# Temporaries of a weight conversion in a PSUM buffer, its last subtraction on VectorE, and a new list schedule

## The chip, the cores and the metric

One core of a Trainium2 chip runs the whole kernel. The metric is the device time of one execution in microseconds. Five engines take part, each with its own instruction queue: TensorE (PE, its weight loads PEld), VectorE (DVE), ScalarE (ACT), GpSimd (POOL) and SyncE (SP), which here issues nearly all DMAs and passes semaphores on.

## What is computed

A convolution whose weights depend on the position, then a small feed-forward layer with a rational activation. All arrays are float32 except for the two weight matrices, whose 64-bit words are loaded as they are and converted in the kernel.

```python
w = exp(weight_gen - max) / (sum + 1e-9)             # (4, 4096, 8 heads, 7 taps)
attn[b, s, h, :] = sum over k of w[b, s, h, k] * x_pad[b, s + k, h, :]   # 8 heads x 24 = 192
h = attn @ w_in                                      # (16384, 192) @ (192, 2048)
P = a0 + a1*h + a2*h**2 + a3*h**3
Q = 1 + |b0|*|h| + |b1|*h**2
out = (P / (Q + 1e-6)) @ w_out                       # (16384, 2048) @ (2048, 192)
```

## The kernel before

The 16384 rows are cut into 32 chunks of 512 rows, the 2048 columns of the inner layer into 8 slots of 256, so 256 slots in all. For each chunk GpSimd makes the seven taps and adds them (`tap`, `tap_add`), TensorE transposes the result into an h buffer (`tr`), ScalarE casts it (`cast`, L645), VectorE subtracts the cast to get the low part (`rest`, L654), and SP copies both to other partitions (`both`, L664 to xd and L670 to xs). Chunk 0 goes a shorter way, with its taps on VectorE.

A slot is then: TensorE's first product into an h buffer (`m1`, L700, 18 matmuls over high and low parts), on ScalarE the absolute value (`v1`, L734), a square (`z1`, L738), a Ln (L751) and an Exp (L754), on VectorE three operations (`d1` L742, `w1` L746, `gg` L758), of which the last writes g and so frees the h buffer, and on TensorE the second product, called gather here (`m2`, L713), in two halves that add into the accumulator acc. Between the two halves a semaphore instruction on SP (`relay`, L775) passes the accumulator on; it stands in SP's queue like a DMA issue. At a chunk's end ScalarE evicts acc (`ev`, L813). PSUM holds three h buffers and acc.

While the first slots run, the weights are still being converted (`unit`): 14 blocks, A0 to A3 and B0, B1 of w_in (512 words a row each) and W0 to W7 of w_out (384 words). A block is loaded as raw; ScalarE takes its magnitude (`ua1`, mag) and its rounding (`ua2`, rnd); VectorE shifts the high words (`ub1`, L393, tile t), joins sign and exponent (`ub2`, L398, tile w), adds the rounding (`ub3`, L403) and clears tiny values (`ub4`, L408), which for the W blocks writes wo. For A and B blocks ScalarE casts w to the high part wh (`uh`, L436) and the low part wl is w minus wh (`uw`, L440), on VectorE for A0 and B0, on GpSimd for the other four. Tiles t and w lie in SBUF, one t and two w. Slots 2j and 2j+1 of chunks 0 and 1 wait for block Aj, slots 0 to 3 and 4 to 7 also for B0 and B1, the gather of slot i for Wi.

The order on each engine is worked out at build time by a list scheduler (`arrange`). Each operation is an `Op` with an engine, a planned duration, a key, what it depends on, the buffers that it takes and uses. At each step every engine proposes, among its operations that can start within `PATIENCE` of its earliest one, that of the lowest key, and the engine that can start first is served. The tables `OFF` (offsets of a slot's or a chunk's steps), `KEY` and `LOADS` (the blocks) set the keys; `PITCH` is the planned time of a slot. An operation of VectorE with `lock=True` is planned as shutting out GpSimd, and GpSimd it. On the chip each engine simply goes through its row of instructions and waits for semaphores.

Of the kernel before, what the change touches and what calls it, by code (L numbers as in the profile page):

```python
# [14 lines left out]
ALU = mybir.AluOpType  # L15
# [6 lines left out]
P = 128  # L22
# [5 lines left out]
N = Q * P  # L28
# [9 lines left out]

BUFS = {
# [3 lines left out]
}  # L43

PITCH = 4.8545
OFF = {
    "g": 13.51, "ex": 4.89, "ln": 3.41, "v": 12.93, "z": 5.73, "d": 7.19, "w1": 3.82, "m2": 3.16,
    "aft": 0.41, "step": 1.43, "cast": 0.61, "rest": -18.71, "dup": 12.06, "lead": 13.14,
    "w": 46.44, "wW": 10.17, "one": -7.23, "ahead": 52.98, "ul": -53.2,
}  # L50
KEY = {
    "B0": -29.4, "A0": -28.0, "W0": 32.8, "A1": 30.0, "W1": 12.93, "W2": 43.45, "W3": 40.29,
    "B1": 40.0, "A2": 50.17, "W4": 52.64, "W5": 52.8, "A3": 52.8, "W6": 62.0, "W7": 69.16,
}
LOADS = (
    "B0", "A0", "W0", "A1", "W1", "W2", "W3", "B1", "A2", "W4", "W5", "A3", "W6", "W7",
# [26 lines left out]
def hand(a, b):  # L83
    if a.land is not None:
        return 0.1
    if a.eng == b.eng:
        return 0.0
    return 0.22 if a.eng == "PE" else 0.08


PATIENCE = 0.346


def arrange(ops, place):
    users, newest = {}, {}
    for i, o in enumerate(ops):
        o.seq = i
        o.left = len(o.deps)
        for d in o.deps:
            d.outs.append((o, True))  # L100
        for t in o.takes:
            if t[0] not in LOOSE:
                if t[0] in newest:
                    newest[t[0]].outs.append((o, False))
                    o.left += 1
                newest[t[0]] = o
        for t in o.takes + o.uses:
            users.setdefault(t, []).append(o)
    engines = ("PE", "ACT", "DVE", "POOL", "SP")
    free = dict.fromkeys(engines, 0.0)  # L110
    ready = {e: [] for e in engines}
    for o in ops:
        if not o.left:
            ready[o.eng].append(o)
    taken = {}
    order = []
    pool_busy = (0.0, 0.0)
    pipe = 0.0

    def room(o):  # L120
        t = 0.0
        for tile_id in o.takes:
            held = taken.setdefault(tile_id[0], [None] * BUFS[tile_id[0]])
            first = None
            for k, past in enumerate(held):
                at = freed(past, o) if past is not None else 0.0
                if at is not None and (first is None or at < first[0]):
                    first = at, k
            if first is None:
                return None  # L130
            t = max(t, first[0])
            place[tile_id] = first[1]
        return t

    def freed(tile_id, o):
        t = 0.0
        for u in users[tile_id]:
            if u.start is None:
                return None
            t = max(t, (u.start + u.land if u.land is not None else u.end) + hand(u, o))  # L140
        return t

    while len(order) < len(ops):
        best = None
        for e in engines:
            found = []
            for o in ready[e]:
                r = room(o)
                if r is not None:
                    found.append((max(free[e], o.ready, r), o))  # L150
            if not found:
                continue
            low = min(s for s, _ in found) + PATIENCE
            s, o = min(
                (x for x in found if x[0] <= low),
                key=lambda x: (
                    x[1].key + (max(0.0, pool_busy[1] - x[0]) * LOCK if x[1].lock else 0.0),
                    x[1].seq,
                ),
            )  # L160
# [37 lines left out]
def kernel(  # L198
# [10 lines left out]
    nc = tc.nc  # L209
# [87 lines left out]
    def sg_():  # L297
# [8 lines left out]
        unit_, inv, sign, op=ALU.mult), [o_r1])  # L306
# [45 lines left out]

    ready_w = {}

    def unit(u):
        kind, j = u[0], int(u[1])
        base = KEY[u]
        t = {}
        width = 2 * D if kind == "W" else U
        cost = 0.75 if kind == "W" else 1.0  # L360
# [28 lines left out]
                out=t["rnd"], in_=t["lo"].bitcast(U32), func=ACTF.Identity, scale=2.0 ** -29)  # L389

        def ub1():
            t["t1"] = tiled(("t1", u), [P, width], I32)
            nc.vector.tensor_scalar(  # L393
                t["t1"], t["hi"], 3, 0x3FFFFFF8, op0=ALU.logical_shift_left, op1=ALU.bitwise_and)

        def ub2():
            t["w"] = tiled(("w", u), [P, width], I32)
            nc.vector.scalar_tensor_tensor(  # L398
                out=t["w"], in0=t["hi"], scalar=-0x40000000, in1=t["t1"], op0=ALU.bitwise_and,
                op1=ALU.bitwise_or)  # L400
# [11 lines left out]
        issue = {"A": 0.9, "B": 0.9, "W": 0.45}[kind]  # L412
        raw, mag, rnd, t1, w = ((k, u) for k in ("raw", "mag", "rnd", "t1", "w"))
        o = op("SP", issue, OFF["ul"] + LOADS.index(u), ul, takes=[raw], land=512.0 * cost)
        p1 = op("ACT", 0.67 * cost, base, ua1, [o], takes=[mag], uses=[raw])
        p2 = op("ACT", 0.66 * cost, base, ua2, [o], takes=[rnd], uses=[raw])
        o = op("DVE", 0.42 * cost, base + 0.5, ub1, [o], takes=[t1], uses=[raw], lock=True)
        o = op("DVE", 0.69 * cost, base + 1.0, ub2, [o], takes=[w], uses=[raw, t1], lock=True)
        o = op("DVE", 0.69 * cost, base + 1.5, ub3, [o, p2], uses=[w, rnd], lock=True)
        o = op("DVE", 0.69 * cost, base + 2.0, ub4, [o, p1], uses=[w, mag], lock=True)  # L420
        if kind == "W":
            ready_w[u] = [o]
            return
# [1 line left out]
        if kind == "A":  # L425
            high, low = (v[:, 0:2, 2 * j:2 * j + 2, :].rearrange("p b n c -> p b (n c)")
                         for v in (wh, wl))
        else:
            high, low = (v[:, 2:3, 4 * j:4 * j + 4, :].rearrange("p b n c -> p b (n c)")
                         for v in (wh, wl))  # L430

        def words_of():
            return t["w"].bitcast(FP32).rearrange("p (b f) -> p b f", b=2 if kind == "A" else 1)
# [2 lines left out]
            nc.scalar.copy(out=high, in_=words_of())  # L436

        def uw():
            eng = nc.vector if u in FAST else nc.gpsimd
            eng.tensor_tensor(low, words_of(), high.bitcast(FP32), op=ALU.subtract)  # L440

        oh = op("ACT", 0.62, base + 3.0, uh, [o], uses=[w])
        if u in FAST:
            ol = op("DVE", 0.69, base + 4.0, uw, [oh], uses=[w], lock=True)
        else:
            ol = op("POOL", 1.27, base + 4.0, uw, [oh], uses=[w])
        ready_w[u] = [oh, ol]

    FAST = ("A0", "B0")
    for u in LOADS:  # L450
        unit(u)

# [371 lines left out]
    for n in range(NSLOT):  # L824
# [3 lines left out]
        slot(n, made[c][0], made[c][1], made[c][2])  # L828

    order = arrange(ops, place)  # L830
    with tc.manual_schedule():
        nc.scalar.preload_act_table_set("natural_log_exp_and_others")
# [136 lines left out]
```

## Time and profile before

| | us |
|---|---|
| median of 3 runs | 1323.15 (1322.0 to 1325.54) |
| the profiled execution | 1321.83 |
| its span, first to last instruction | 1320.0 |

| engine | busy us | share of the span |
|---|---|---|
| TensorE matmuls | 1268.7 | 96% |
| VectorE | 1156.0 | 88% |
| ScalarE | 1140.9 | 86% |
| GpSimd | 895.3 | 68% |

The shares are averages over a head of some 100 us, in which chunk 0 is prepared and the weights are converted, and a long even part. A share says what an engine did, not what it waited for; for the latter there are the rows of single instructions with their idle time. Operations of one line can have two sizes (384 and 512 words), so a mean over a line mixes them.

### The profile page before, as it was taken

How to read it: one execution, taken by the hardware profiler on the slowest of the kernel's cores; microseconds unless marked ns; L12 is line 12 of the kernel's file. 1: busy time of each engine (PE TensorE's matmuls, PEld its weight loads, DVE VectorE, ACT ScalarE, POOL GpSimd, SP SyncE). 2: the span in 40 equal slices, each digit the busy share in tenths (PEclk: the TensorE clock that was granted, in tenths of full speed). 3: DMA queues.
4: the chain of work that ended last, by engine and by line, in shares of the span. 5: the costliest groups of instructions: out<-in, count | busy, mean ns of one | idle time of the engine just before them, and what ended most of it. 6: DMA issues, size and time to landing. Idle time of an engine off the chain costs nothing.

```text
span 1320.0 us, 30705 instructions
## 1 busy us (share of the span) xinstructions
PE 1268.7 (96%) x13082; PEld 1150.2 (87%) x13082; DVE 1156.0 (88%) x975; ACT 1140.9 (86%) x1162; POOL 895.3 (68%) x582
## 2 busy tenths in 40 slices
PE   7549999999999999999999999999999999999998
PEld 5438998999999999999999899999899999999997
DVE  7998988888889989888888898988888988889874
ACT  4649989988899899989989899998899899889985
POOL 2585898766767876666787666688766668866300
PEclk9869999999999999999999999999999999999999
DMA  7322122232112222211222222123222212221100
GB/s 186 98 69 65 51 67 75 79 79 78 48 43 67 78 78 79 79 44 39 75 78 79 79 49 62 47 79 78 79 78 50 54 56 78 78 78 46 45 13 15
DMA packets 46291, 89.07 MB, mean 67 GB/s; under 512 B 5426, under 2 KB 27976, under 8 KB 46148
## 3 DMA queue, kind: packets, MB, share of 16 engines
q1 hardware_dynamic: 45860, 87.05, 24.2%
q8 instruction: 104, 1.70, 0.5%
q14 instruction: 39, 0.32, 0.1%
q10 hardware_dynamic: 288, 0.00, 0.0%
HBM read 41.40 MB, written 12.58 MB: 41 GB/s over the span
## 4 chain that ended last, share of the span: by engine, by line
PE 87%; DVE 6%; ACT 3%; SPq 2%; issue 1%; DMA 1%; ACTq 0%; DVEq 0%
PE acc L713 48%; PE h L700 38%; PE h L632 1%; SPq L664 1%; ACT av L754 1%; DVE w L403 1%; DVE av L742 1%; DVE w L398 1%; DVE t L393 1%; DMA x<-in_x_dram 1%; DVE g L758 1%; DVE wo L408 1%; ACT av L751 1%; ACT av L734 0%; SPq L670 0%
## 5 line engine op out<-in xcount | busy, mean ns | idle before, releaser
L713 PE MATMUL acc<-wo,g 64*128 64x192 f32 x8192 | 723.1, 325 | 14.9 <-DVE g L758 10.1
L713 PEld LDWEIGHTS acc<-wo,g 64*128 64x128 f32 x8192 | 680.8, 187 | 48.0 <-SPq L775 12.1
L742 DVE SCALAR_TENSOR_TENSOR av<-av,cf 128x1024 f32<-128x1024 f32 x256 | 428.6, 1674 | 93.8 <-ACT av L734 90.8
L564 POOL TENSOR_TENSOR at<-at,pr 128x768 f32<-128x768 f32 x155 | 384.1, 2478 | 11.7
L758 DVE SCALAR_TENSOR_TENSOR g<-h,ab,av 128x1024 f32<-128x1024 f32 x256 | 326.8, 1277 | 38.3 <-ACT av L754 37.9
L751 ACT ACTIVATE av<-av,c 128x1024 f32<-128x1024 f32 x256 | 294.1, 1149 | 47.5 <-DVE av L742 44.2
L746 DVE SCALAR_TENSOR_TENSOR h<-pv,cf,h 128x1024 f32<-128x1024 f32 x256 | 326.7, 1276 | 0.2 <-ACT pv L738 0.2
L734 ACT ACTIVATE av<-h 128x1024 f32<-128x1024 f32 x256 | 260.4, 1017 | 74.2 <-PE h L700 72.7
L552 POOL TENSOR_TENSOR pr<-x,wn 128x768 f32<-128x768 f32 x186 | 315.9, 1698 | 0.0
L738 ACT ACTIVATE pv<-h,cf,rt 128x1024 f32<-128x1024 f32 x256 | 307.0, 1199 | 0.0
L754 ACT ACTIVATE av<-av 128x1024 f32<-128x1024 f32 x256 | 269.4, 1052 | 1.7
L700 PE MATMUL h<-xm,wh 64*128 64x512 f32 x1024 | 240.0, 459 | 23.9 <-DVE xm L654 13.0
L700 PE MATMUL h<-xs,wh 64*128 64x512 f32 x1024 | 209.1, 396 | 2.0 <-DMA xs<-xm 2.0
L700 PE MATMUL h<-xd,wh 64*128 64x512 f32 x1024 | 207.1, 394 | 0.0
L700 PEld LDWEIGHTS h<-xm,wh 64*128 64x128 f32 x1024 | 101.0, 187 | 35.4 <-DVE xm L654 13.3
L700 PEld LDWEIGHTS h<-xs,wh 64*128 64x128 f32 x1024 | 101.7, 187 | 23.6 <-DMA xs<-xm 3.2
L700 PEld LDWEIGHTS h<-xd,wh 64*128 64x128 f32 x1024 | 100.4, 186 | 19.7
L505 POOL TENSOR_TENSOR e<-wgt,mx 128x224 f32<-128x224 f32 x31 | 18.9, 611 | 134.2 <-DVE mx L501 134.1
L700 PE MATMUL h<-xs,wl 64*128 64x512 f32 x512 | 104.1, 394 | 0.0
L700 PE MATMUL h<-xd,wl 64*128 64x512 f32 x512 | 103.6, 394 | 0.0
L700 PE MATMUL h<-xm,wl 64*128 64x512 f32 x512 | 103.0, 392 | 0.0
L515 POOL TENSOR_SCALAR mx<-mx,cf 128x32 f32<-128x32 f32 x31 | 9.3, 301 | 124.9 <-DVE mx L512 124.7
(91 smaller groups left out, 631.3 us busy)
## 6 DMA issues: line engine op xcount, KB each, us to landing
x<-in_x_dram SPq DMA_DIRECT2D x24, 960.0 KB, 6.2
xs<-xm SPq DMA_DIRECT2D x64, 256.0 KB, 3.6
xd<-xm SPq DMA_DIRECT2D x124, 128.0 KB, 2.4
out_dram<-ob SPq DMA_DIRECT2D x32, 384.0 KB, 4.6
wgt<-in_weight_gen_dram SPq DMA_DIRECT2D x32, 112.0 KB, 4.0
raw<-in_moe_w_in_dram SPq DMA_DIRECT2D x12, 256.0 KB, 3.7
raw<-in_moe_w_out_dram SPq DMA_DIRECT2D x8, 384.0 KB, 3.6
x<-in_x_dram SPq DMA_DIRECT2D x4, 768.0 KB, 4.7
```

The costliest lines, as they stand in the source:

```text
L505: (nc.vector if early else nc.gpsimd).tensor_tensor(t["e"], t["wg"], t["mx"].to_broadcast([P, QH, K]), op=ALU.subtract)
L552: eng.tensor_tensor(dst.rearrange("p q (h g) -> p q h g", g=G), t["x"][:, k:k + Q, :].rearrange("p q (h g) -> p q h g", g=G), t["wn"][:, k ...
L564: eng.tensor_tensor(at, at, term, op=ALU.add)
L700: nc.tensor.matmul(h[:, f, :], w[half, b_, i, :], v[half, part, 0:N], start=k == 0, stop=k == 8, skip_group_check=True)
L713: done.append(nc.tensor.matmul(acc[:, bank, q_ * D:(q_ + 1) * D], g[half, f, seat(q) * P:(seat(q) + 1) * P], wo[half, 2 * i + f, :], start ...
L734: nc.scalar.activation(out=t["v"], in_=flat(t["h"]), func=ACTF.Abs)
L738: nc.scalar.activation(out=t["z"], in_=flat(t["h"]), func=ACTF.Square, scale=steep, bias=shift)
L742: nc.vector.scalar_tensor_tensor(out=t["v"], in0=t["v"], scalar=rb, in1=t["v"], op0=ALU.add, op1=ALU.mult)
L746: nc.vector.scalar_tensor_tensor(out=flat(t["h"]), in0=t["z"], scalar=lift, in1=flat(t["h"]), op0=ALU.add, op1=ALU.mult)
L751: nc.scalar.activation(out=t["v"], in_=t["v"], func=ACTF.Ln, bias=c0)
L754: nc.scalar.activation(out=t["v"], in_=t["v"], func=ACTF.Exp, scale=-1.0)
L758: nc.vector.scalar_tensor_tensor(out=flat(t["g"]), in0=flat(t["h"]), scalar=a0, in1=t["v"], op0=ALU.add, op1=ALU.mult)
```

## The change

The two tiles t and w of the conversion become two halves of one PSUM tile, which takes one of the three h buffers from the start until the last block is converted (`seat_tmp`, `tmp`). There is one w where there were two. The low parts of all six A and B blocks are subtracted on VectorE. The conversion's operations no longer carry `lock`; the shift and the first two ScalarE operations are planned in another order and length. In `arrange`, where the operation about to be placed has `lock` and GpSimd could start within 0.12 us of it, GpSimd's is placed first. `PITCH`, `PATIENCE` and the tables have other numbers, which move rows on all engines.

```diff
-    "pv": 3, "g": 4, "ob": 2, "mag": 2, "rnd": 2, "t1": 1, "w": 2,
+    "pv": 3, "g": 4, "ob": 2, "mag": 2, "rnd": 2, "t1": 1, "w": 1,
...
-PITCH = 4.8545
+PITCH = 4.8729
...
-    "aft": 0.41, "step": 1.43, "cast": 0.61, "rest": -18.71, "dup": 12.06, "lead": 13.14,
+    "aft": 4.99, "step": 2.35, "cast": -1.03, "rest": -13.5, "dup": 13.03, "lead": 14.38,
...
-PATIENCE = 0.346
+PATIENCE = 0.302
...
+            heads[e] = (s, o)
...
+        if o.lock and "POOL" in heads and heads["POOL"][0] <= s + 0.12:
+            s, o = heads["POOL"]
...
+    TMP = ("h", "tmp")
+
+    def seat_tmp():
+        T[TMP] = tiled(TMP, [P, 2, N])
+
+    o_tmp = op("DVE", 0.01, -400.0, seat_tmp, takes=[TMP])
+
+    def tmp(k, width):
+        return T[TMP][:, k, 0:width].bitcast(I32)
...
-            t["t1"] = tiled(("t1", u), [P, width], I32)
+            t["t1"] = tmp(0, width)
...
-            t["w"] = tiled(("w", u), [P, width], I32)
+            t["w"] = tmp(1, width)
...
-        p1 = op("ACT", 0.67 * cost, base, ua1, [o], takes=[mag], uses=[raw])
-        p2 = op("ACT", 0.66 * cost, base, ua2, [o], takes=[rnd], uses=[raw])
-        o = op("DVE", 0.42 * cost, base + 0.5, ub1, [o], takes=[t1], uses=[raw], lock=True)
-        o = op("DVE", 0.69 * cost, base + 1.0, ub2, [o], takes=[w], uses=[raw, t1], lock=True)
...
+        p2 = op("ACT", 0.66 * cost, base, ua2, [o], takes=[rnd, mag], uses=[raw])
+        p1 = op("ACT", 0.67 * cost, base, ua1, [o, p2], uses=[raw, mag])
+        o = op("DVE", 0.6 * cost, base + 0.5, ub1, [p2, o_tmp], takes=[t1], uses=[raw, TMP])
+        o = op("DVE", 0.69 * cost, base + 1.0, ub2, [o], takes=[w], uses=[raw, t1, TMP])
...
-            eng = nc.vector if u in FAST else nc.gpsimd
-            eng.tensor_tensor(low, words_of(), high.bitcast(FP32), op=ALU.subtract)
+            nc.vector.tensor_tensor(low, words_of(), high.bitcast(FP32), op=ALU.subtract)
```

The lines of the changed kernel are 8 to 16 further down: L406, L411, L416, L421 are the four conversion operations, L449 and L452 high and low part, L742, L746, L759, L762 are ScalarE's and L750, L754, L766 VectorE's operations of a slot, L653 and L821 cast and eviction.

ScalarE, the first slots after the start, before. h_320, h_351, h_383 and h_424 are the h tiles of slots 0 to 3, the av tiles theirs in the same order.

```order
L734 ACTIVATE av_370<-h_320 128x1024
L738 ACTIVATE pv_377<-h_320,cf_67,rt_74 128x1024
L734 ACTIVATE av_381<-h_351 128x1024
L738 ACTIVATE pv_402<-h_351,cf_67,rt_74 128x1024
L751 ACTIVATE av_370<-av_370,c0_68 128x1024
L754 ACTIVATE av_370<-av_370 128x1024
L734 ACTIVATE av_412<-h_383 128x1024
L384 ACTIVATE mag_418<-raw_298 128x512
L388 ACTIVATE rnd_422<-raw_298 128x512
L751 ACTIVATE av_381<-av_381,c0_68 128x1024
L754 ACTIVATE av_381<-av_381 128x1024
L734 ACTIVATE av_459<-h_424 128x1024
```

The same place after; h_318, h_350 and h_398 are the tiles of slots 0, 1 and 2.

```order
L742 ACTIVATE av_369<-h_318 128x1024
L746 ACTIVATE pv_376<-h_318,cf_67,rt_74 128x1024
L742 ACTIVATE av_379<-h_350 128x1024
L759 ACTIVATE av_369<-av_369,c0_68 128x1024
L762 ACTIVATE av_369<-av_369 128x1024
L746 ACTIVATE pv_391<-h_350,cf_67,rt_74 128x1024
L759 ACTIVATE av_379<-av_379,c0_68 128x1024
L762 ACTIVATE av_379<-av_379 128x1024
L517 ACTIVATE e_382<-e_382 128x224
L401 ACTIVATE rnd_423<-raw_296 128x512
L397 ACTIVATE mag_425<-raw_296 128x512
L742 ACTIVATE av_438<-h_398 128x1024
```

The activation of slot 2 has moved from behind the Exp of slot 0 to behind that of slot 1, the square of slot 1 from ahead of the first Ln to behind the first Exp.

VectorE, conversion of block A2 (raw_310), with W4 (raw_344) and a g of slot 3 among it, before. The low part isn't in this queue.

```order
L393 TENSOR_SCALAR t1_545<-raw_310 128x512
L398 SCALAR_TENSOR_TENSOR w_548<-raw_310,t1_545 128x512
L403 ISA w_548<-w_548,rnd_515 128x1024
L408 SCALAR_TENSOR_TENSOR w_548<-mag_511,w_548 128x512
L393 TENSOR_SCALAR t1_556<-raw_344 128x384
L758 SCALAR_TENSOR_TENSOR g_560<-h_424,ab_65,av_459 128x1024
L398 SCALAR_TENSOR_TENSOR w_566<-raw_344,t1_556 128x384
```

The same block (raw_311) after. h_82 is the PSUM tile of the temporaries.

```order
L406 TENSOR_SCALAR h_82<-raw_311 128x512
L411 SCALAR_TENSOR_TENSOR h_82<-raw_311,h_82 128x512
L416 ISA h_82<-h_82,rnd_466 128x1024
L421 SCALAR_TENSOR_TENSOR h_82<-mag_520,h_82 128x512
L406 TENSOR_SCALAR h_82<-raw_344 128x384
L766 SCALAR_TENSOR_TENSOR g_580<-h_442,ab_65,av_484 128x1024
L452 TENSOR_TENSOR wl_70<-h_82,wh_69 128x2x256
```

The operations write and read h_82 in place of t1 and w, and the subtraction to wl stands in VectorE's queue, behind the g.

ScalarE at the end of a chunk in the even part, before: xm is written by the cast, ob by the eviction.

```order
L738 ACTIVATE pv_6087<-h_6039,cf_67,rt_74 128x1024
L751 ACTIVATE av_6074<-av_6074,c0_68 128x1024
L645 CAST xm_6110<-h_6090 128x768
L813 COPY ob_6132<-acc_5722 128x768
L754 ACTIVATE av_6074<-av_6074 128x1024
L734 ACTIVATE av_6159<-h_6113 128x1024
```

The same place after.

```order
L746 ACTIVATE pv_6059<-h_6012,cf_67,rt_74 128x1024
L653 CAST xm_6081<-h_6062 128x768
L759 ACTIVATE av_6046<-av_6046,c0_68 128x1024
L821 COPY ob_6109<-acc_5697 128x768
L762 ACTIVATE av_6046<-av_6046 128x1024
L742 ACTIVATE av_6132<-h_6088 128x1024
```

The cast has moved ahead of the Ln, and the Ln stands between cast and eviction.

## Rows read from the trace of the kernel before

**Rows 1.** Busy us by stretch: PE, PEld, DVE, ACT, POOL; granted clock; DMA.

```profile
28.00:100.00 72.00, 36.92 (x262) 28.87 (x262) 67.69 (x67) 39.68 (x51) 49.71 (x32) 0.72 0.33 94
...
47.50:51.50 4.00, 3.96 (x18) 3.41 (x20) 4.00 (x4) 2.70 (x4) 3.66 (x3) 0.50 0.00 0
```

**Rows 2.** Instructions of TensorE in time order: start, us; bracket: idle before, releaser.

```profile
47.54 0.80 PE L700 MATMUL h<-xm,wh 64*128 64x512 f32 x2 [8.93 <-DVE g L758]
...
51.52 3.39 PE L713 MATMUL acc<-wo,g 64*128 64x192 f32 x32
...
72.12 4.96 PE L713 MATMUL acc<-wo,g 64*128 64x192 f32 x32 [9.30 <-DVE g L758]
...
95.12 0.79 PE L700 MATMUL h<-xm,wh 64*128 64x512 f32 x2 [13.04 <-DVE xm L654]
```

**Rows 3.** The same view of ScalarE, columns as in group 2.

```profile
38.62 0.55 ACT L384 ACTIVATE mag<-raw 128x384 f32<-128x384 f32 x1 [1.57 <-DVE wo L408]
...
108.10 1.02 ACT L734 ACTIVATE av<-h 128x1024 f32<-128x1024 f32 x1 [2.04 <-PE h L700]
```

**Rows 4.** Busy time of the operations on tile w, then on its shift.

```profile
28.00:100.00 72.00, 33.56 (x33) 2.44 (x4) 5.78 (x4) 0.72 0.33 94
...
28.00:100.00 72.00, 9.09 (x10) 0.72 0.33 94
```

**Rows 5.** Operations on w and t, whole run: count, ns minimum/median/maximum.

```profile
L403 DVE CUSTOM_DVE_ANT_0 w<-w,rnd x14: 544/685/2070, 10.8 to 97.4; 128x768 uint16<-128x768 uint16 x8, 128x1024 uint16<-128x1024 uint16 x6
...
L408 DVE SCALAR_TENSOR_TENSOR w<-mag,w x6: 684/692/1855, 17.0 to 80.4; 128x512 f32<-128x512 f32 x6
...
L440 POOL TENSOR_TENSOR wl<-w,wh x4: 1272/1469/1574, 31.2 to 81.8; 128x512 fp32r<-128x512 f32 x4
...
L393 DVE TENSOR_SCALAR t<-raw x14: 347/428/1961, 9.5 to 85.3; 128x384 int32<-128x384 int32 x8, 128x512 int32<-128x512 int32 x6
```

**Rows 6.** The slot's three VectorE lines, the same columns.

```profile
L742 DVE SCALAR_TENSOR_TENSOR av<-av,cf x256: 1185/1526/2948, 42.5 to 1300.2; 128x1024 f32<-128x1024 f32 x128
...
L746 DVE SCALAR_TENSOR_TENSOR h<-pv,cf,h x256: 1270/1276/1290, 43.7 to 1302.6; 128x1024 f32<-128x1024 f32 x128
...
L758 DVE SCALAR_TENSOR_TENSOR g<-h,ab,av x256: 1269/1275/1286, 46.1 to 1304.3; 128x1024 f32<-128x1024 f32 x128
```

**Rows 7.** VectorE's instructions by form: count | busy us, mean ns | idle.

```profile
L651 DVE TENSOR_TENSOR xm<-h,xm 128x512 fp32r<-128x512 f32 x1 | 0.7, 684 | 0.0
...
L600 DVE COPY pv<-h 128x256 f32<-128x256 f32 x1 | 0.4, 425 | 0.1
```

**Rows 8.** The same of ScalarE, from the page.

```profile
L734 ACT ACTIVATE av<-h 128x1024 f32<-128x1024 f32 x256 | 260.4, 1017 | 74.2 <-PE h L700 72.7
```

**Rows 9.** The chain that ended last, in time order: start, us.

```profile
165.05 2.60 PE acc L713 x32
...
167.65 2.09 PE h L700 x18
```

**Rows 10.** The transposes of six chunks on TensorE, columns as in group 2.

```profile
351.35 0.66 PE L632 MATMUL h<-ident,as 128*128 128x128 f32 x4
...
390.01 0.66 PE L632 MATMUL h<-ident,as 128*128 128x128 f32 x4
...
892.50 0.66 PE L632 MATMUL h<-ident,as 128*128 128x128 f32 x4
...
931.03 0.66 PE L632 MATMUL h<-ident,as 128*128 128x128 f32 x4
...
970.28 0.66 PE L632 MATMUL h<-ident,as 128*128 128x128 f32 x4
...
1241.44 0.66 PE L632 MATMUL h<-ident,as 128*128 128x128 f32 x4
```

**Rows 11.** Two chunks' copies xd on SP's queue: start, us from first issue.

```profile
354.25 3.36 SPq L664 DMA_DIRECT2D xd<-xm  x4
...
934.44 3.43 SPq L664 DMA_DIRECT2D xd<-xm  x4
```

More of the change, by code (lines that the diff above doesn't have):

```diff
@@ L40 @@
     "x": 3, "wgt": 3, "mx": 3, "e": 2, "wn": 2, "pr": 3, "at": 2, "xm": 2, "xd": 2, "xs": 2, "av": 4,
[1 row of a table removed]
[1 row of a table added]
     "h": 3, "acc": 1, "raw": 4, "as": 2,
 }
-PITCH = 4.8545
+PITCH = 4.8729
 OFF = {
-    "g": 13.51, "ex": 4.89, "ln": 3.41, "v": 12.93, "z": 5.73, "d": 7.19, "w1": 3.82, "m2": 3.16,
-    "aft": 0.41, "step": 1.43, "cast": 0.61, "rest": -18.71, "dup": 12.06, "lead": 13.14,
-    "w": 46.44, "wW": 10.17, "one": -7.23, "ahead": 52.98, "ul": -53.2,
+    "g": 12.72, "ex": 3.33, "ln": 5.25, "v": 13.04, "z": 5.74, "d": 7.0, "w1": 3.82, "m2": 3.16,
+    "aft": 4.99, "step": 2.35, "cast": -1.03, "rest": -13.5, "dup": 13.03, "lead": 14.38,
+    "w": 45.09, "wW": 10.62, "one": -7.23, "ahead": 52.98, "ul": -53.2,
 }
 KEY = {
-    "B0": -29.4, "A0": -28.0, "W0": 32.8, "A1": 30.0, "W1": 12.93, "W2": 43.45, "W3": 40.29,
-    "B1": 40.0, "A2": 50.17, "W4": 52.64, "W5": 52.8, "A3": 52.8, "W6": 62.0, "W7": 69.16,
+    "B0": -29.4, "A0": -28.0, "W0": 32.8, "A1": 30.0, "W1": 12.93, "W2": 43.45, "W3": 10.63,
+    "B1": 41.25, "A2": 50.17, "W4": 51.8, "W5": 52.8, "A3": 52.8, "W6": 63.24, "W7": 76.41,
 }
@@ L143, in arrange @@
     while len(order) < len(ops):
-        best = None
+        best, heads = None, {}
         for e in engines:
@@ L414, in unit @@
         o = op("SP", issue, OFF["ul"] + LOADS.index(u), ul, takes=[raw], land=512.0 * cost)
-        p1 = op("ACT", 0.67 * cost, base, ua1, [o], takes=[mag], uses=[raw])
-        p2 = op("ACT", 0.66 * cost, base, ua2, [o], takes=[rnd], uses=[raw])
-        o = op("DVE", 0.42 * cost, base + 0.5, ub1, [o], takes=[t1], uses=[raw], lock=True)
-        o = op("DVE", 0.69 * cost, base + 1.0, ub2, [o], takes=[w], uses=[raw, t1], lock=True)
-        o = op("DVE", 0.69 * cost, base + 1.5, ub3, [o, p2], uses=[w, rnd], lock=True)
-        o = op("DVE", 0.69 * cost, base + 2.0, ub4, [o, p1], uses=[w, mag], lock=True)
+        p2 = op("ACT", 0.66 * cost, base, ua2, [o], takes=[rnd, mag], uses=[raw])
+        p1 = op("ACT", 0.67 * cost, base, ua1, [o, p2], uses=[raw, mag])
+        o = op("DVE", 0.6 * cost, base + 0.5, ub1, [p2, o_tmp], takes=[t1], uses=[raw, TMP])
+        o = op("DVE", 0.69 * cost, base + 1.0, ub2, [o], takes=[w], uses=[raw, t1, TMP])
+        o = op("DVE", 0.69 * cost, base + 1.5, ub3, [o, p2], uses=[w, rnd, TMP])
+        o = op("DVE", 0.69 * cost, base + 2.0, ub4, [o, p1], uses=[w, mag, TMP])
         if kind == "W":
@@ L438, in uw @@
         def uw():
-            eng = nc.vector if u in FAST else nc.gpsimd
-            eng.tensor_tensor(low, words_of(), high.bitcast(FP32), op=ALU.subtract)
[L442 to L446, printed above, removed]
+            nc.vector.tensor_tensor(low, words_of(), high.bitcast(FP32), op=ALU.subtract)
+        oh = op("ACT", 0.62, base + 3.0, uh, [o], uses=[w, TMP])
+        ol = op("DVE", 0.69, base + 4.0, uw, [oh], uses=[w, TMP])
         ready_w[u] = [oh, ol]
-    FAST = ("A0", "B0")
     for u in LOADS:
```

## The prediction

> **What bounds the kernel now.** I began with the busy time by slices and went from there to the stretch of 28 to 100 us. In the middle of the run TensorE never stops: one slot is a first product of 2.09 us and a gather of 2.60 us [rows 9], and a chunk of eight slots with its transposes takes 38.53 us from one set of transposes to the next (892.50 to 931.03 [rows 10]). Nothing that VectorE or GpSimd does there moves the end. In 28 to 100 us it is the other way round: VectorE is busy for 67.69 of 72 us, TensorE for 36.92 [rows 1]. That is where 14 blocks of weights are converted while the first slots already run. TensorE's own waits say the same: 8.93 us for a g of VectorE, later 9.30 us for another, then 13.04 us for the low part of chunk 1 [rows 2], and the activation of slot 8 starts only at 108.10 us [rows 3]. From about there TensorE is full, so whatever the head saves comes off the end one for one.
>
> Why is VectorE so slow in the head? The conversion has four operations on each block. Undisturbed they take 0.55 us (the 384-word blocks) or 0.69 us (512 words), and the shift 0.35 or 0.42 us; the longest of the same operations take 1.86 to 2.07 us [rows 5]. All their tiles lie in SBUF. The slot work shows who disturbs: the operation with SBUF tiles alone (L742) runs from 1.185 to 2.948 us, while L746 and L758, which have the PSUM tile h among their operands, stay at 1.27 to 1.29 us over 256 instructions each [rows 6], beside a GpSimd that works all the while. So a VectorE operation with one operand in PSUM and one in SBUF isn't held up by GpSimd.
>
> **The change, part by part.**
> *Temporaries in PSUM.* In 28 to 100 us VectorE spends 33.56 us on 33 operations on w and 9.09 us on 10 shifts, 42.65 us in all [rows 4]. Undisturbed these are 22 of 0.55, 11 of 0.69, 7 shifts of 0.35 and 3 of 0.42: 23.4 us. The stretching is worth 19.2 us, on an engine that sets the pace. In the changed kernel each of these operations has one operand in PSUM and at most one tensor input in SBUF, the form that [rows 6] shows undisturbed: minus 19.2 us. The shift loses its fast form: a copy out of PSUM takes 0.425 us for 256 words and a subtraction 0.684 us for 512 [rows 7], so 0.56 and 0.68 us; 7 times 0.21 and 3 times 0.26 is plus 2.3 us. The other three keep their price: 0.684 us with PSUM [rows 7] against 0.684 at least without [rows 5].
>
> [...]
>
> *Low parts on VectorE.* Four subtractions leave GpSimd, where they took 1.27 to 1.57 us each [rows 5], for VectorE at 0.684 us [rows 7]: plus 2.7 us. What GpSimd saves counts for nothing: it stands idle for 22 of the 72 us [rows 1].
>
> Net on VectorE: 19.2 less 2.3 less 2.7, 14.2 us. Before 28 us, three longer shifts (0.8 us) and two operations of block A1 now ahead of the low part of chunk 0 delay the first product by up to 2 us. I cost that at nothing: slot 0's activation stands on ScalarE behind a conversion that waits for VectorE until 38.62 us [rows 3], and this wait shrinks by more.
>
> *One of three h buffers gone until the last block is converted.* Two are left for slots 0 to 9. Slot 2's first product must now wait for slot 0's g; the first pair of order listings shows the activation of slot 2 (h_398) moved behind both Exps, where before it stood behind one. VectorE then stands idle where the rows between that g and the next slot's first operation don't fill a first product and an activation. [...] The activation adds 1.02 us [rows 8]. From the order I count the VectorE rows in between. Slot 0's g to slot 2: a 1.28, a 1.28, shift, reduction and a 0.55, some 4.2 us against 5.2: 1.0 idle. Low part of A2 to slot 4: eight conversion operations, 5 us, against 4.4 to 7.4 (half a gather stands in between too): 0 to 2.4. Slot 4's g to slot 6: 3.7 against 5.1: 1.4. Slot 6's g to slot 8: 4.0 against 3.2 to 5.0: 0 to 1.0. Together 2.4 to 5.8 us. I take 3.8, a little under the middle, since for slots 4 and 8 a gather has just run ahead of the product. The head gains 14.2 less 3.8, 10.4 us.
>
> *Order.* In later chunks the changed list puts the cast of the transposes ahead of a Ln on ScalarE (third pair of listings). After the cast SP issues the copies xd and xs, and the semaphore that passes the accumulator from one half of a gather to the other stands behind them in SP's queue. Where the cast comes after the Ln and the copies take 3.43 us to issue, the chunk takes 39.25 us (931.03 to 970.28), 0.72 more than the 38.53 of the chunk ahead of it; in a chunk whose cast already comes first, 3.36 us cost 0.13 (351.35 to 390.01) [rows 10, 11]. Between 390.01 and 1241.44 [rows 10] lie 22 chunks, 3.8 us above 38.53 each, and the change should return most of that: 3.2 us, between 0 and 3.8. The eviction of the accumulator moves behind the Ln. The chunk at 351.35 has this order too, so its 0.13 us is the most I charge for that, and nothing where the copies issue faster: TensorE has a first product to do meanwhile. The rule that lets GpSimd go first and the longer pitch only sort rows: cost nothing while TensorE is full.
>
> **Sum.** The profiled execution took 1321.83 us (span 1320.0), 1.3 below the median of 1323.15. 1321.83 less 10.4 less 3.2 is 1308.2, on the scale of the median 1309.5 us.
>
> **Rivals.**
> [...]
> 2. *The two buffers cost all they can (slower).* Blocks are converted one after the other through one set of temporaries, so an operation that waits for ScalarE's rounding or cast holds the slot work behind it on VectorE. If nothing covers the product and the activation, five round trips (into slots 2, 3, 4, 6 and 8) at 3.98 + 1.02 us are 25 us against 17.4 gained: 1323.15 + 7.6, 1331. It turns slower from 3.5 us idle in each of the five. Against it: in 28 to 100 us VectorE stood for 4.3 us in all [rows 1] and there is more than one block to convert for each slot.
> 3. *The stretching stays (slower or no change).* Three of the four operations still read raw, rnd or mag in SBUF. If GpSimd holds those up as before, 5.0 us are added, 3.8 lost in waits and 3.2 returned: 1328.8. L746 and L758 read one SBUF tile too and speak against it.
> 4. *Each PSUM operand costs a little.* The shortest L742 is 0.085 us below the shortest L746 of the same size [rows 6]. If that is the price of PSUM, 47 operations cost 4.0 us: about 1313.5. For it speaks that one row, against it the pair at 0.684 us. [...]
> 5. *Nothing uncovered.* If conversion fills every gap, 3.8 us come back: about 1305.7.
>
> **How the numbers follow.** The forecast has 0.62, rivals 1 to 5 have 0.10, 0.06, 0.07, 0.05 and 0.10. A measurement of this kernel can tell about 0.3%, 4 us, from no change, so faster means below 1319.2. The forecast and rivals 1, 4 and 5 lie there, 0.87, less 0.02 for sizes missed: 0.85. Rivals 2 and 3 may stop half-way: 0.06 within, 0.09 slower. The range takes rival 5 with full return of the chunks' excess and something for shorter gaps, 1302, up to rival 1 with the long waits, 1318.
>
> **What would show it.** The conversion operations at one length each, none above 0.75 us (rival 1: the add at 0.95 to 1.3; rival 3: lengths up to 2 us). Less than 5 us idle on VectorE in the head for an activation; slot 4's first product near 68 us instead of 77 (where the gather of 4.96 us from 72.12 ends [rows 2]), slot 8's activation near 97 instead of 108. TensorE's start again after fewer than 8 us each time. In the chunks: 38.5 to 38.7 us, few waits for SP's semaphore. Wrong would be a head that ends as late as before with VectorE idle, or chunks longer than 38.53 us throughout.

## The result, and the profile after

The changed kernel takes 1304.04 us (median of 4 runs, 1303.29 to 1305.3) against 1323.0 us, a ratio of 0.9855 with a 95% interval of 0.9838 to 0.9872. That is 19.0 us less; 13.6 were forecast, and the time lies in the range of 1302 to 1318. The two profiled executions stand 17.3 us apart (spans of 1320.0 and 1302.7); the one before lay 1.2 us under the median of its runs, the one after 0.5 above (1304.49), which makes up the other 1.7.

The busy time of 28 to 100 us, as in [rows 1], and then that of the four conversion lines (shift, combine, add, scale) and the low parts on VectorE in the same stretch (us, count; what follows is granted clock and DMA), as in [rows 4]:

```profile
28.00:100.00 72.00, 51.15 (x398) 43.18 (x400) 65.36 (x79) 50.20 (x61) 47.79 (x32) 0.78 0.37 102
...
28.00:100.00 72.00, 6.52 (x11) 0.78 0.37 102
...
28.00:100.00 72.00, 6.54 (x11) 0.78 0.37 102
...
28.00:100.00 72.00, 6.05 (x10) 0.78 0.37 102
...
28.00:100.00 72.00, 5.95 (x10) 0.78 0.37 102
...
28.00:100.00 72.00, 2.73 (x4) 0.78 0.37 102
```

VectorE is about as busy as before, but TensorE now does 51.15 us of work in the stretch, where it did 36.92. 42 conversion operations take 25.06 us; 43 took 42.65 [rows 4]. The lengths of each kind over the whole run say why (ns: shortest, median, longest; columns as in [rows 5]):

```profile
L406 DVE TENSOR_SCALAR h<-raw x14: 548/561/694, 9.6 to 94.5; 128x384 int32<-128x384 int32 x8, 128x512 int32<-128x512 int32 x6
L411 DVE SCALAR_TENSOR_TENSOR h<-raw,h x14: 553/562/696, 10.3 to 96.3; 128x384 int32<-128x384 int32 x8, 128x512 int32<-128x512 int32 x6
L416 DVE CUSTOM_DVE_ANT_0 h<-h,rnd x14: 551/567/700, 11.2 to 100.0; 128x768 uint16<-128x768 uint16 x8, 128x1024 uint16<-128x1024 uint16 x6
L421 DVE SCALAR_TENSOR_TENSOR wo<-mag,h x8: 545/554/555, 31.6 to 100.6; 128x384 f32<-128x384 f32 x8
L452 DVE TENSOR_TENSOR wl<-h,wh x6: 672/678/693, 19.6 to 79.8; 128x512 fp32r<-128x512 f32 x6
```

No operation is above 0.70 us; before, the longest of the kinds in [rows 5] were 1.86 to 2.07 us. TensorE's long waits in the head, as in [rows 2], and the first product of slot 4 (start, us; in brackets the idle time before and what ended it):

```profile
44.75 0.79 PE L708 MATMUL h<-xm,wh 64*128 64x512 f32 x2 [6.15 <-DVE g L766]
...
65.89 2.93 PE L721 MATMUL acc<-wo,g 64*128 64x192 f32 x16 [5.00 <-DVE g L766]
...
68.36 0.88 PE L708 MATMUL h<-xm,wh 64*128 64x512 f32 x2
...
81.83 0.79 PE L708 MATMUL h<-xm,wh 64*128 64x512 f32 x2 [7.09 <-DVE g L766]
```

The three waits add up to 18.2 us, where 8.93, 9.30 and 13.04 were 31.3 [rows 2]: 13 us less. Slot 8's activation on ScalarE, at 108.10 before [rows 3], starts at 96.26:

```profile
96.26 1.02 ACT L742 ACTIVATE av<-h 128x1024 f32<-128x1024 f32 x1 [1.17 <-PE h L708]
```

Then the chunks, as in [rows 10]. First the fifth set of transposes in the kernel before:

```profile
235.41 0.66 PE L632 MATMUL h<-ident,as 128*128 128x128 f32 x4
```

Then in the changed kernel the fifth and the ninth set; the three at 993.0, 1031.36 and 1069.81, which stand for the usual spacing; and the last one:

```profile
222.97 0.66 PE L640 MATMUL h<-ident,as 128*128 128x128 f32 x4
...
376.62 0.66 PE L640 MATMUL h<-ident,as 128*128 128x128 f32 x4
...
993.00 0.65 PE L640 MATMUL h<-ident,as 128*128 128x128 f32 x4
...
1031.36 0.66 PE L640 MATMUL h<-ident,as 128*128 128x128 f32 x4
...
1069.81 0.66 PE L640 MATMUL h<-ident,as 128*128 128x128 f32 x4
...
1224.40 0.66 PE L640 MATMUL h<-ident,as 128*128 128x128 f32 x4
```

A usual chunk takes 38.36 and 38.45 us in turn, 38.41 on average, where every usual one took 38.53. The 22 chunks that took 851.43 us between 390.01 and 1241.44 [rows 10] now take 847.78 (376.62 to 1224.4): 3.65 us less. At the fifth set of transposes (235.41 before, 222.97 after) the kernel is 12.4 us ahead; that is the head. 12.4, 3.65, 0.95 in the four chunks between and 0.3 at the end make up the 17.3.

### The profile page after: what moved, and what is told of

It reads as the page before. It is cut to its first block, busy times and chain, and to the rows that moved or that the text cites. A ratio compares the mean times of both kernels' runs of the same rounds, so it can differ in the third digit from the quotient of the medians.

```text
span 1302.7 us, 30683 instructions
## 1 busy us (share of the span) xinstructions
PE 1266.2 (97%) x13082; PEld 1154.6 (89%) x13082; DVE 1178.8 (90%) x979; ACT 1135.5 (87%) x1162; POOL 863.3 (66%) x578
## 4 chain that ended last, share of the span: by engine, by line
PE 88%; DVE 3%; POOL 3%; ACT 2%; SPq 1%; issue 1%; DMA 1%; DVEq 0%; ACTq 0%; POOLq 0%
PE acc L721 49%; PE h L708 38%; PE h L640 1%; POOL pr L560 1%; POOL at L572 1%; SPq L672 1%; DMA x<-in_x_dram 1%; DVE g L766 0%; ACT av L742 0%; PE h L643 0%; SPq L678 0%; DVE av L750 0%; DVE h L411 0%; DVE xm L662 0%; ACT av L759 0%
## 5 line engine op out<-in xcount | busy, mean ns | idle before, releaser
L750 DVE SCALAR_TENSOR_TENSOR av<-av,cf 128x1024 f32<-128x1024 f32 x256 | 464.3, 1814 | 57.7 <-ACT av L742 57.5
L560 POOL TENSOR_TENSOR pr<-x,wn 128x768 f32<-128x768 f32 x186 | 364.8, 1961 | 0.1
L766 DVE SCALAR_TENSOR_TENSOR g<-h,ab,av 128x1024 f32<-128x1024 f32 x256 | 327.2, 1278 | 37.2 <-ACT av L762 33.2
L742 ACT ACTIVATE av<-h 128x1024 f32<-128x1024 f32 x256 | 260.2, 1016 | 82.4 <-PE h L708 78.5
L754 DVE SCALAR_TENSOR_TENSOR h<-pv,cf,h 128x1024 f32<-128x1024 f32 x256 | 326.7, 1276 | 0.8 <-ACT pv L746 0.8
L759 ACT ACTIVATE av<-av,c 128x1024 f32<-128x1024 f32 x256 | 293.0, 1145 | 37.1 <-DVE av L750 37.1
L572 POOL TENSOR_TENSOR at<-at,pr 128x768 f32<-128x768 f32 x155 | 312.5, 2016 | 12.2
L746 ACT ACTIVATE pv<-h,cf,rt 128x1024 f32<-128x1024 f32 x256 | 306.9, 1199 | 0.0
L762 ACT ACTIVATE av<-av 128x1024 f32<-128x1024 f32 x256 | 270.2, 1056 | 3.3
L578 POOL TENSOR_TENSOR as<-at,pr 128x512 f32<-128x512 f32 (+1 forms) x62 | 86.7, 1401 | 2.4
```

What stands on the lines that cost most here:

```text
L560: eng.tensor_tensor(dst.rearrange("p q (h g) -> p q h g", g=G), t["x"][:, k:k + Q, :].rearrange("p q (h g) -> p q h g", g=G), t["wn"][:, k ...
L572: eng.tensor_tensor(at, at, term, op=ALU.add)
L578: eng.tensor_tensor(t["as"][:, start:start + Q * (hi - lo)].rearrange("p (q d) -> p q d", q=Q), at[:, :, lo:hi], term[:, :, lo:hi], op=ALU ...
L742: nc.scalar.activation(out=t["v"], in_=flat(t["h"]), func=ACTF.Abs)
L746: nc.scalar.activation(out=t["z"], in_=flat(t["h"]), func=ACTF.Square, scale=steep, bias=shift)
L750: nc.vector.scalar_tensor_tensor(out=t["v"], in0=t["v"], scalar=rb, in1=t["v"], op0=ALU.add, op1=ALU.mult)
```

## The experiments

The times of before beside them were 1323.0, 1323.4 and 1323.9 us in the three sets of runs (e1 to e4, e5 to e8, e9 to e12).

**Is it the place in PSUM, or the order?** e1 changes one line and keeps the order:

```
-        T[TMP] = tiled(TMP, [P, 2, N])
+        T[TMP] = sb.tile([P, 2, N], FP32, tag="tmp", bufs=1, name="tmp")
```

> The changed kernel with its order kept instruction for instruction, but the two temporaries of the conversion lie in SBUF; the h buffer stays reserved, so slots 0 to 9 still have two. Theory (GpSimd stretches VectorE operations whose tensors all lie in SBUF, and PSUM frees them): the 56 conversion operations, 34.4 us in the changed kernel, go back towards the 50.3 us they had before, with the longest near 2 us, less the 3.5 us that the shift in SBUF gives back: 9 to 13 us lost, 1313 to 1317. Rival (the new order, with GpSimd first, keeps the two engines apart, and PSUM does little): all operations stay under 0.75 us and the time is 1301 to 1305.

Measured: 1320.42 us (ratio to before 0.997 to 0.999). The same lines as above, in e1:

```profile
L406 DVE TENSOR_SCALAR tmp<-raw x14: 352/418/2008, 9.6 to 112.3; 128x384 int32<-128x384 int32 x8, 128x512 int32<-128x512 int32 x6
L411 DVE SCALAR_TENSOR_TENSOR tmp<-raw,tmp x14: 550/685/2047, 10.0 to 114.1; 128x384 int32<-128x384 int32 x8, 128x512 int32<-128x512 int32 x6
L416 DVE CUSTOM_DVE_ANT_0 tmp<-tmp,rnd x14: 544/692/2174, 10.9 to 117.8; 128x768 uint16<-128x768 uint16 x8, 128x1024 uint16<-128x1024 uint16 x6
L452 DVE TENSOR_TENSOR wl<-tmp,wh x6: 672/728/2305, 19.5 to 97.4; 128x512 fp32r<-128x512 f32 x6
```

The stretching is back, on the low parts too, and 16.4 of the 19.0 us are gone, more than expected. The expectation took 3.5 us off for the shift's form in SBUF, but the 50.3 us that it started from are those of the kernel before and hold that form already. Measured, the 56 operations take 53.7 us, and the six low parts 6.05 us instead of 4.08. The order alone does not keep the engines apart.

**Is it GpSimd?** e2 is e1 with the middle taps on a quarter of the rows in chunks 1 to 3 (m counts the rows of Q = 4; the product of a tap is cut by m too):

```
+                m = 1 if c in THIN and 0 < k < K - 1 else Q
...
-                    eng.tensor_tensor(at, at, term, op=ALU.add)
+                    m = 1 if c in THIN else Q
+                    eng.tensor_tensor(at[:, 0:m], at[:, 0:m], term[:, 0:m], op=ALU.add)
```

> As the run before, with GpSimd's work in the head made small: of the seven taps of chunks 1 to 3 the middle five and their sums are computed on a quarter of the rows only (the output of these chunks is left wrong by that). Order and instruction count are the same. Theory: without GpSimd beside them the conversions in SBUF take 0.35 to 0.75 us each, some 31 to 34 us in all, and the time falls to 1300 to 1305, at or under the changed kernel. Rival (ScalarE or the DMA traffic does the stretching): lengths and time stay as in the run before.

Measured: 1304.13 us. GpSimd is busy for 29.63 us in 28 to 100 us, where e1 had 52.23:

```profile
28.00:100.00 72.00, 50.23 (x390) 42.37 (x392) 66.20 (x80) 49.74 (x61) 29.63 (x32) 0.78 0.36 102
...
L407 DVE TENSOR_SCALAR tmp<-raw x14: 348/414/747, 9.6 to 95.3; 128x384 int32<-128x384 int32 x8, 128x512 int32<-128x512 int32 x6
L422 DVE SCALAR_TENSOR_TENSOR wo<-mag,tmp x8: 547/558/559, 34.1 to 101.3; 128x384 f32<-128x384 f32 x8
L453 DVE TENSOR_TENSOR wl<-tmp,wh x6: 673/804/1905, 19.6 to 80.9; 128x512 fp32r<-128x512 f32 x6
```

The 56 operations take 36.7 us, after 53.7 in e1. Some are still long (a low part of 1.905 us, a combine of 1.77), with the first and the last tap of a chunk still whole. ScalarE is busy for 49.74 us and the DMAs for a share of 0.36, about as in the changed kernel (50.20 and 0.37) and more than in e1 (36.82 and 0.31), so it is GpSimd that stretches VectorE's operations with SBUF tiles alone. The kernel before shows the two cases for the add on 128x1024: 2.07 us beside GpSimd's taps, 0.69 us where GpSimd stood idle (5.69 us, up to 81.78):

```profile
64.42 2.13 POOL L564 TENSOR_TENSOR at<-at,pr 128x768 f32<-128x768 f32 x1
...
65.03 2.07 DVE L403 CUSTOM_DVE_ANT_0 w<-w,rnd 128x1024 uint16<-128x1024 uint16 x1
...
66.51 1.93 POOL L552 TENSOR_TENSOR pr<-x,wn 128x768 f32<-128x768 f32 x1
...
79.57 0.69 DVE L403 CUSTOM_DVE_ANT_0 w<-w,rnd 128x1024 uint16<-128x1024 uint16 x1
...
81.78 1.42 POOL L440 TENSOR_TENSOR wl<-w,wh 128x512 fp32r<-128x512 f32 x1 [5.69 <-ACT wh L436]
```

**Does VectorE set the pace of the head?** e3 takes the four low parts off it again:

```
+                dst = t["f"] = sb.tile([P, width], FP32, tag=f"f{u}", bufs=1, name="f")
...
-            nc.vector.tensor_tensor(low, words_of(), high.bitcast(FP32), op=ALU.subtract)
+            eng = nc.gpsimd if "f" in t else nc.vector
+            eng.tensor_tensor(low, words_of(), high.bitcast(FP32), op=ALU.subtract)
```

> The changed kernel with the low parts of A1, A2, A3 and B1 back on GpSimd: the last of the four VectorE operations writes its result to an SBUF tile of its own, from which ScalarE casts and GpSimd subtracts. VectorE loses 4 operations of 0.68 us. Theory (VectorE sets the pace in the head): 2.7 us faster, 1301 to 1302. Rival (the low parts queue behind GpSimd's taps, and the first products wait for them): 1304 to 1312, with TensorE waiting for a GpSimd operation.

Measured: 1301.11 us, 2.9 under the changed kernel. Slot 16 starts 2.4 us earlier than in the changed kernel; no first product waits for GpSimd. This version, ahead of both kernels, has the lowest median of all (e10, which adds padding to it, has 1301.17). Its low parts:

```profile
L459 POOL TENSOR_TENSOR wl<-f,wh x4: 1267/1278/1597, 31.7 to 78.9; 128x512 fp32r<-128x512 f32 x4
```

**What does the lost h buffer cost?** e8 is the kernel before with one buffer held and unused (a tile HOLD of h, taken first and used by each conversion's shift and scale).

> The kernel before, temporaries in SBUF, but one of the three h buffers is kept out of use until the last block is converted; its scheduler sorts the work anew. This prices the lost buffer alone. Prediction: 3.8 us of waits (2.4 to 5.8), 1325 to 1329. Rival (conversion fills every gap): 1322 to 1324. Rival (nothing covers the product and the activation): 1335 or more.

Measured: 1323.62 us, no difference from before (ratio 0.9993 to 1.0012). Taken alone that says "costs nothing". The transposes say otherwise (fifth set, and two later):

```profile
239.16 0.66 PE L635 MATMUL h<-ident,as 128*128 128x128 f32 x4
...
393.31 0.66 PE L635 MATMUL h<-ident,as 128*128 128x128 f32 x4
...
1241.86 0.66 PE L635 MATMUL h<-ident,as 128*128 128x128 f32 x4
```

The head ends at 239.16 instead of 235.41: 3.75 us later, as much as the 3.8 of the forecast, but not by the waits that the forecast counted. Up to slot 8 VectorE waited for the activation of a slot for 2.51 us in the kernel before (one wait) and for 3.33 us in e8: 0.28, 0.40 and this one:

```profile
104.74 1.71 DVE L745 SCALAR_TENSOR_TENSOR av<-av,cf 128x1024 f32<-128x1024 f32 x1 [2.65 <-ACT av L737]
```

In the new order the stretching lies on other operations: the 56 conversion operations take 53.8 us instead of 50.3, VectorE's first operations (av<-av,cf) of slots 0 to 7 together 12.3 us instead of 15.5, and one more g (1.2 us) and a wait of 0.75 us for an Exp stand ahead of slot 8's. So 3.75 us is what the buffer costs with this list, stretching included. Then the 22 chunks take 848.55 us instead of 851.43, and most of the loss is given back. In e8's newly sorted list the cast starts 0.91 to 0.95 us after the transposes in all of them (1.6 us in most before), and SP's copies start 2.72 to 2.77 us after the transposes (here the chunk at 894.76):

```profile
897.48 2.55 SPq L667 DMA_DIRECT2D xd<-xm  x4
```

In the kernel before they start 3.41 us after them (934.44 for the chunk at 931.03 [rows 10, 11]). So the chunk part of the forecast is seen here by itself, 2.9 of at most 3.8 us.

**Is it the order in the chunks?** e4 uses the old offsets from chunk 6 on:

```
+        OFF = OLD if c >= FROM else NEW
```

> The changed kernel, but from chunk 6 on the table of offsets of the kernel before sorts the work (cast, rest, eviction, the slot's parts). The head stays. Theory of the prediction (the cast ahead of Ln takes SP's copies out of the gather's way): the excess over the usual chunk comes back, 1 to 3 us, 1305 to 1307; if the 0.12 us by which a usual chunk became shorter (38.53 to 38.41) is also the order's, another 2.7 us, up to 1309. Rival (the shorter chunk comes from where tiles lie in memory): usual chunks stay at 38.41 us.

Measured: 1312.97 us, 8.9 slower than the changed kernel, more than either theory gave. The cast still comes early (0.95 us after the transposes), but SP has another transfer ahead of the copies:

```profile
847.68 0.34 SPq L833 DMA_DIRECT2D out_dram<-ob  x1
848.13 2.56 SPq L680 DMA_DIRECT2D xd<-xm  x4
850.79 1.25 SPq L686 DMA_DIRECT2D xs<-xm  x2
```

The store of the output waits for the accumulator's eviction, and the copies, which start 2.73 us after the transposes in the changed kernel, start 3.70 us after those at 844.43. So does the chunk grow: e4's usual one takes 38.59 us, longer than in either kernel, which neither theory had:

```profile
844.43 0.66 PE L648 MATMUL h<-ident,as 128*128 128x128 f32 x4
...
883.02 0.66 PE L648 MATMUL h<-ident,as 128*128 128x128 f32 x4
```

What counts is when the copies end. In the usual chunk the last one (xs) has been issued 7.3 us after the transposes before, 6.6 in the changed kernel and 7.6 in e4. In both kernels a chunk has its usual length while that end lies before some 7.4 us; beyond that, and in e4 always, it grows by as much as the end is late: 39.25 us with an end at 8.20 (931.03 before), 38.97 with 7.98 (530.58 in the changed kernel), 40.23 with 9.24 (1154.74 in e4). TensorE's waits for the semaphore behind the copies show it (us in total, times, longest, from 150 us on), first in the changed kernel, then in e4:

```profile
PE acc L721 <- SPq L783: 1.0, 3, 0.4
...
PEld acc L721 <- SPq L783: 6.1, 12, 0.8
```

```profile
PE acc L729 <- SPq L792: 7.1, 9, 1.6
...
PEld acc L729 <- SPq L792: 19.5, 32, 2.0
```

The end of the copies is the lever; cast and eviction both move their start. The run mixes two tables, so its 8.9 us is not the worth of the change's own order.

**Why is a usual chunk shorter?** In e4 first products of 2.19 us still alternate with longer ones, though the order is another. In the changed kernel they go by chunk: 2.19 us (840.79 to 842.98) in even ones, 2.23 (867.48 to 869.71) in odd ones:

```profile
840.79 0.53 PE L708 MATMUL h<-xm,wh 64*128 64x512 f32 x2
...
842.98 1.46 PE L721 MATMUL acc<-wo,g 64*128 64x192 f32 x16
...
867.48 0.53 PE L708 MATMUL h<-xm,wh 64*128 64x512 f32 x2
...
869.71 2.76 PE L721 MATMUL acc<-wo,g 64*128 64x192 f32 x32
```

Before, nearly all took 2.22 or 2.23 (these are times from the start of a first product to the start of what follows). Even and odd chunks use two sets of xm, xd and xs. A first guess was the distance of xs from xd; an unused tile changes it (e5; in e6 with e3's edit, in e7 in the kernel before):

```
+            if c in (1,):
+                sb.tile([P, 768], FP32, tag=f"gap{c}", bufs=1, name="gap")
             xs = t["xs"] = tiled(XS, [P, 2, N], FP32R)
```

> The changed kernel with an unused SBUF tile of 3 KB per partition between xd and xs of the second set of chunk buffers; nothing else. In the changed kernel the first products of even chunks take 2.19 us, of odd chunks 2.22 to 2.23 us; in the kernel before all take the longer time. The first set, used by even chunks, happens to have the tile at (3 KB) between xd and xs, the second has xs directly behind xd, as both sets have in the kernel before. Theory (where xs lies against xd sets the time of a product): all products 2.19 us, 0.24 us less in each of some 15 odd chunks, 3.6 us in all, about 1300.5. Rival (the parity comes from something else, such as the other buffers of two): nothing changes, 1304.

> The low parts on GpSimd and the gap together. If the two gains are independent, 1301.1 less 3.6, about 1297.5; if the gap does nothing, 1301.

> The kernel before with a gap of 3 KB between xd and xs of both sets of buffers; nothing else. Theory: all first products 2.19 us, a usual chunk 38.28 us instead of 38.53, some 7 us in all, about 1316. Rival: unchanged, 1323.

Measured: 1303.89, 1302.16 and 1323.84 us; the products did not change. That guess fell. The second was the start of the tiles within 256 bytes (128 bytes more, ahead of xm: the second set in e9 and e10, the first and with it the second in e11):

```
+            if c == 1:
+                sb.tile([P, 32], FP32, tag="pad", bufs=1, name="pad")
             t["xm"] = tiled(XM, [P, 2, N + 2 * P], FP32R)
```

> The changed kernel with an unused tile of 128 bytes per partition ahead of the second set of xm, xd, xs; nothing else. The gap of 3 KB changed nothing: the first products of odd chunks still take 2.22 us, of even ones 2.19. What still differs between the sets is the start of the tiles: the set of even chunks starts 32 bytes behind a multiple of 256 (xm at 112928), that of odd chunks 160 bytes behind one (xm at 182944), as both do in the kernel before (118176, 190112). Theory (a first product is 0.03 us longer where its tiles start 160 bytes behind a multiple of 256): all products 2.19 us, a usual chunk 38.3 us, 0.24 us less in some 15 odd chunks, 3.6 us, about 1300.4. Rival (not the place in memory at all): 1304, as with the gap.

> The low parts on GpSimd and the shift of 128 bytes together, a version that might beat both kernels: 1301.1 less 3.6, about 1297.5, if the shift works; 1301 to 1302 if not.

> The kernel before with an unused tile of 128 bytes ahead of the first set of xm, xd, xs, which shifts both sets; nothing else. The first set then starts 32 bytes behind a multiple of 512, the second 288 bytes behind one, so both stand 32 bytes behind a multiple of 256. Theory with 256: all products 2.19 us, a usual chunk 38.28 us, some 7 us in all, 1316. If 512 is what counts (288 in the fast set of the changed kernel): only every other chunk gains, 1319.5. Rival: unchanged, 1323.

Measured: e11 takes 1318.6 us, a ratio of 0.9953 to 0.9977, so 128 unused bytes make the kernel before 5.3 us faster (3.1 by the spans of the profiled pair, 1320.0 and 1316.9). Its usual chunk, 851.62 to 890.02, is 38.4 us, in even and odd chunks alike:

```profile
851.62 0.66 PE L632 MATMUL h<-ident,as 128*128 128x128 f32 x4
...
890.02 0.66 PE L632 MATMUL h<-ident,as 128*128 128x128 f32 x4
```

e9's usual chunks are 38.36 to 38.38 us, its time 1302.85 (1300.31 to 1305.54), too close to 1304.04 to tell apart; e10's 1301.17 is e3's. So the start within 256 bytes matters, for the two starts that were run, and 512 does not. The sizes were overrated: the products of both sets now take 2.20 us in the mean, not 2.19, and the chunk 38.36, not 38.28. What takes the rest isn't settled, nor why the start matters.

**Do the tables carry the gain?** e12 has the changed code with all tables of before.

> The changed code (temporaries in PSUM, low parts on VectorE, one h buffer held, GpSimd first) with the tables, pitch and patience of the kernel before. Theory (the undisturbed conversion is the gain, the tables only sort): the head ends 9 to 13 us earlier than before, and with the old order in the chunks the total is 1308 to 1314. Rival (the tables carry the gain): 1319 to 1324.

Measured: 1306.72 us (ratio 0.9855 to 0.9886). With tables made for another kernel the edit brings 17.2 us, by the before of its own set; its usual chunk is 38.44 us, so most of the shorter chunk (0.09 of 0.12 us) comes with the code, not with the tables. By stretches: the fifth transposes come at 221.99, 13.4 us earlier than before and 1.0 earlier than in the changed kernel, and the 22 chunks (376.08 to 1226.72) take 850.64 us, 0.8 less than before. So the new tables bring nothing to the head and some 2.9 us to the chunks. The rule that lets GpSimd go first is in every run with the changed code, so no run prices it by itself.

## Why the prediction was right, and where its sizes were off

*Conversion in PSUM: right.* Forecast for 28 to 100 us were 23.4 + 2.3 = 25.7 us for 43 operations; 42 took 25.06. The shift lost its fast form (0.548 us at least instead of 0.347), the add kept its time (0.551 to 0.700 us, where its shortest was 0.544, so rival 1, an add at 0.95 to 1.3 us, falls), and e1 and e2 show the cause. No run shows the half-speed add from which the range has its end of 1318; the longest add was 0.700 us. Rival 3 falls with them: raw, rnd and mag in SBUF didn't bring the stretching back. Rival 4 falls too: the shortest combine is 0.553 us where it was 0.546 in SBUF, 0.007 us more, and the slot operation L742, whose shortest 1.185 us was that rival's only row, has a shortest of 1.270 now (L750), while that of L754, with PSUM, is 1.205: the difference has changed sides, so it was no price of PSUM.

*Low parts: right.* Four at 0.68 us, 2.73 us, and without them e3's slot 16 starts 2.4 us earlier.

*Two h buffers: mis-sized.* The sum took 3.8 us as additional idle time of VectorE. That e8 is 3.75 us late is no proof of it, but luck: there the waits grew by 0.8 us only. The working has 5.2 and 5.1 us for a product and an activation, which no row shows: a product of 3.98 us (47.54 to 51.52 [rows 2], at a granted clock of 0.50 [rows 1]) and an activation of 1.02 make 5.0, and its lower ends take the 2.09 us of [rows 9], where the granted clock was 1.00. In the changed kernel the first products at 44.75 and 81.83, after TensorE had stood for 6.15 and 7.09 us, took 3.98 us each at a granted clock of 0.50, and the one at 68.36, behind a gather, 2.84 us at 0.75. Before, VectorE already waited for an activation once in that part:

```profile
100.43 2.27 DVE L742 SCALAR_TENSOR_TENSOR av<-av,cf 128x1024 f32<-128x1024 f32 x1 [2.51 <-ACT av L734]
```

In the changed kernel this wait is gone, and these have come:

```profile
50.05 1.44 DVE L750 SCALAR_TENSOR_TENSOR av<-av,cf 128x1024 f32<-128x1024 f32 x1 [1.44 <-ACT av L742]
...
72.49 2.88 DVE L750 SCALAR_TENSOR_TENSOR av<-av,cf 128x1024 f32<-128x1024 f32 x1 [1.17 <-ACT av L742]
...
87.13 1.28 DVE L750 SCALAR_TENSOR_TENSOR av<-av,cf 128x1024 f32<-128x1024 f32 x1 [1.80 <-ACT av L742]
```

4.4 us, 4.8 with two short ones, against 2.5: about 2 more, not 3.8. That is the mis-sized term of the head: 12.4 us measured, 10.4 forecast. Two things that the forecast didn't have nearly cancel: the first operations of slots 0 to 7, with SBUF tiles alone, take 13.85 us instead of 15.49, and one more g (1.2 us) stands ahead of slot 8's. Rival 2 (five uncovered round trips) falls: no wait is above 1.8 us. Rival 5 (nothing uncovered), the nearest by its time, falls as well: the waits are there.

*Order in the chunks: the mechanism holds, the term doesn't.* The forecast had 3.2 us from the copies alone. The cast does come earlier (0.91 us after the transposes instead of 1.61, the copies at 2.73 instead of 3.41), and e8 and e4 show that the end of the copies decides. But the excess of the 22 chunks over the usual one fell only from 3.8 to 2.8 us (847.78 less 22 times 38.41), because some copies now took longer to issue: xd up to 3.91 us, where the longest before were 3.62, and xs 2.4 in chunks where xd took its usual 2.56:

```profile
533.31 3.89 SPq L672 DMA_DIRECT2D xd<-xm  x4
537.31 1.25 SPq L678 DMA_DIRECT2D xs<-xm  x2
...
538.67 2.87 PE L721 MATMUL acc<-wo,g 64*128 64x192 f32 x32 [0.32 <-SPq L783]
```

That chunk (530.58 to 569.55) takes 38.97 us. The other 2.6 us (22 times 0.12) come in the main from where the tiles lie in SBUF, which the forecast didn't have at all: the changed code moved xm, xd and xs. With no set of fast products the usual chunk is 38.53 us, with two 38.36 (e9, e11); one set would give 38.45 if its share is half, and 38.41 were measured. So this part, 3.65 us against 3.2, was met by luck: 1.0 us came from the copies. What sets the issue time of a copy (2.55 us mostly, up to 3.9) stays open.

*The total.* 13.6 us were forecast and 19.0 measured. The head makes 2.0 of the difference, the 22 chunks 0.4, the four chunks ahead of them and the end, which the forecast left out, 1.25, and the place of the two profiled executions among their runs 1.7.

*The points to look for.* Slot 4's first product was put near 68 us (68.36), slot 8's activation near 97 (96.26), TensorE's restarts under 8 us (6.15, 5.00, 7.09), VectorE's waits for activations under 5 us: all so. Chunks of 38.5 to 38.7 us were not.

## What to carry to other kernels

Where VectorE sets the pace and GpSimd works beside it, look at the spread of one operation's length: if it runs from 0.55 to 2 us while operations with a PSUM operand keep one length (1.27 to 1.29 us [rows 6]), try an intermediate tile in PSUM; here it gave back all the excess of the operations that use it (56 of them took 50.3 us before and 34.5 after) and was worth a buffer. Waits that a change brings are set against those that it takes away, on the same engine and stretch. A run whose time is unchanged (e8) can hold a loss and a gain of nearly equal size: compare by stretches. And a measured size that equals the forecast one, as e8's 3.75 us, shows the mechanism only where the rows have the forecast waits too.

## What the runs showed of the hardware

Beside a GpSimd that is busy for 52 of 72 us (e1), VectorE's add on SBUF tiles took 0.54 to 2.17 us and the low part 0.67 to 2.31; with one operand in PSUM the conversion's operations stayed within 0.03 us of their shortest at each size (changed kernel). Not expected: a first product on TensorE took 2.19 to 2.20 us where its tiles xm, xd and xs started 32 bytes behind a multiple of 256, and 2.22 to 2.23 us where they started 160 bytes behind one (no other start was run); 128 bytes of padding took 0.4% off the kernel before.
